# Long-convolution block: the shift's taps as 32-column products, a first stage without turns, and an inverse that overwrites the spectrum

## The chip, the core and the metric

The kernel runs on one core of one Trainium2 chip. The metric is the device time of one execution in microseconds (us). The kernel before takes 249.34 us (median of 3 runs, 249.3 to 249.93). The engines are PE (TensorE, with PEld for its weight loads), DVE (VectorE), ACT (ScalarE), POOL (GpSimd) and SP, which issues most transfers.

## The reference, cut to what matters

```python
def _A_ref(q, k, v, shift_k, ssm_k, ssm_D):          # q is layernorm(x)
    k_pad = jnp.pad(k, ((0, 0), (ks - 1, 0), (0, 0)))                  # ks = 4, S = 2048, D = 512
    k_shift = sum over t of k_pad[:, t:t + S, :] * shift_k[:, ks - 1 - t]
    kv = k_shift * v
    y = irfft(rfft(kv, 2 * S) * rfft(ssm_k, 2 * S))[:, :S, :]          # a causal convolution per channel
    return q * (y + kv * ssm_D)

def _B_ref(x, w1, b1, w2, b2):                        # an MLP, 512 -> 1376 -> 512
    return gelu(layernorm(x) @ w1 + b1) @ w2 + b2

x = A_q
for _ in range(2):
    x = x + _A_ref(layernorm(x), k, v, shift_k, ssm_k, ssm_D)
    x = x + _B_ref(layernorm(x), w1, b1, w2, b2)
```

The convolution y depends on k, v, shift_k, ssm_k and ssm_D alone, so both layers use the same y. The kernel computes it once.

## The kernel before, in words

The program has two parts. The **head** computes y and the first MLP group's first product; the **steady part** runs 8 groups (two layers of four) of 4 x 128 tokens, each as 44 products `ph` (L735), their gelu on ACT (L737) and 44 products `po` (L769). Only the head is changed, apart from names and from which token stands on which partition.

In the head the 2048 tokens are split into 32 high values a and 64 low values b. A transform over a (32 points, odd frequencies k = 0..31) comes first, then a twiddled transform over b for each k. The steps have names that the text uses; each product step fills one of four PSUM buffers `p` of 128x1024 numbers, and its evacuation (the same name with an `e`) copies that buffer to SBUF on ACT (L215) or DVE (L217):

- `kT` (L439) turns three of the four channel groups of k on PE, channels to partitions. `kv` (L521) then applies the four taps as products with diagonal matrices DG: 6 steps of 32 products, each with all 128 columns of the array; the turned k is the stationary operand, so tokens come out on partitions. `kvm` (L527) multiplies by v on DVE. The fourth channel group gets its taps on POOL instead (L453, L455, L460, L464).
- `U..S` (L303) is the transform over a of u = kv, 16 products of 256 columns for each of four channel groups. Its result must be turned before the second transform: `U..T`, 16 PE transposes a step (L335) for three groups, and two transposing transfers (L282) for the fourth.
- `KS` (L390) and `K2` (L403) are the same two transforms of ssm_k. KS uses whole products, 4 a step; K2 uses products with 64 rows in pairs (rows 0 to 63 and 64 to 127), 8 a step. The swapped copy of the spectrum that the complex product needs is made by 8 transfers (`sa`, `sb`, SBUF to SBUF).
- `X` (L551) is the second transform of u, `T` (L566) the product with the spectrum on DVE into buffers T, and `V` (L575) the inverse over k2, with T as the stationary operand.
- The inverse over k needs the result turned once more: two channel groups on PE (`TC`, `TD`, L610), two by transposing transfers `Z` (L622). `Y` (L642) is the last product, 32 products of 512 columns with the matrix GP.
- The tail: for the first group of tokens g (L669, L670) gates and adds on DVE, h (L237 to L243) takes statistics, p (L249) the power on POOL, b (L254) applies them, LT (L650) turns, and M (L698, gelu in L706) is the first MLP product, in three units of 1, 1 and 2 token blocks.

The order on every engine is written by hand: the string ORDER lists all steps as `name.engine` and PSUM slot, and each engine's instructions are emitted in that order, so an engine waits at its next step even if a later one is ready. Transfers are issued in the same way from SP's queue. `wm` steps (L420) are products on a table, which keep PE busy.

Of the kernel before, what the change touches and what calls it, by code (L numbers as in the profile page):

```python
# [9 lines left out]
BF16 = mybir.dt.bfloat16  # L10
# [8 lines left out]
lSK.S wm2.P2 bS.P2 wm0.P1 bSe.A dg0.D dg1.A dg2.A lk0.S lk1.S lh1.S kT0.P2 bSK.P1 bSKe.A kT0e.D kT1.P0 kT2.P3 lh113.S lb1.S lx0.S kT1e.D kT2e.A kT3.P1 wm1.P0 bB.P2 bBe.A lv0.S s00.A lv1.S kT3e.D kv10.P3 kvm10.D kv00.P1 U1S0.P30 kv01.P2 kvm00.D U1S1.P1 U0S0.P01 U1S0e.D lK01.S kg0.G kv11.P3 lK00.S kg1.G U0S0e.A kvm01.D U0S1.P0 s01.G U0S1e.A U0S3.P2 U1S1e.D kvm11.D U0S3e.A kv20.P1 kd0.P0 lK11.S lK10.S kvm20.D kd0e.A U1S3.P3 U0S2.P2 U1S3e.A U0S2e.D KS11.P0 KS11e.A KS01.P1 KS30.P3 KS01e.A lW.S KS00.P2 KS00e.A KS30e.D KS10.P0 KS31.P1 KS10e.D kv21.P3 kvm21.D KS31e.A kd4.P1 kd4e.A KS20.P0 KS21.P2 KS20e.A KS70.P1 KS21e.D KS51.P3 KS41.P0 KS70e.A KS51e.A KS60.P2 KS60e.A KS41e.D KS40.P1 KS61.P3 KS40e.D lX.S KS71.P0 KS50.P2 U1S2.P1 KS71e.D KS61e.A KS50e.A U1S2e.A U2S0.P32 U2S0e.D K25.P0 K25e.A K27.P2 K24.P1 K24e.A K23.P3 K21.P0 K21e.A K27e.D K26.P2 U2S1.P1 K26e.A K23e.D U2S1e.D K20.P3 K28.P0 K20e.A K22.P2 K22e.A K212.P1 K28e.D K215.P3 K215e.A lM.S K212e.D sa1.S sb1.S sa0.S K214.P0 K29.P2 K29e.A K213.P1 U0T0.P3 K214e.D K213e.A K210.P0 K210e.A sb0.S K211.P2 U0T1.P1 s02.D K211e.A U2S3.P0 U0T0e.D U2S3e.A U0T1e.D ka1.G kg2.G ka2.G kg3.G X00.P30 ka3.G kgm.G U3S0.P21 U3S0e.D U2S2.P1 X00e.A X01.P01 lH.S U2S2e.A U1T0.P3 U3S1.P2 T00.D0 U3S3.P1 X01e.A U1T1.P0 sb3.S U1T0e.D X10.P30 U3S1e.A U3S3e.A sa3.S X02.P22 T01.D1 X10e.A U2T0.P1 sb2.S U1T1e.D T10.D2 U3S2.P3 U2T0e.D X02e.A sa2.S X12.P01 V00.P2 U3S2e.A T02.D0 V10.P30 X12e.A X03.P10 V00e.A X03e.A V01.P0 V01e.A X20.P22 T12.D2 X20e.A U3T0.S V12.P1 X11.P01 X11e.A V10e.D lx.S V02.P3 U2T1.P2 T03.D1 X13.P00 T20.D2 V12e.A V02e.A T11.D0 V03.P1 U2T1e.D X13e.A V03e.A X30.P32 T13.D1 V11.P0 X30e.A V11e.D X23.P21 V13.P1 X23e.A U3T1.S V13e.A T30.D0 X22.P30 X22e.A T23.D1 V20.P01 X21.P22 ly.S X21e.A V20e.A V30.P12 X32.P31 T22.D2 T21.D0 X31.P20 V22.P0 X32e.A V21.P3 X31e.A V30e.D X33.P12 V22e.A Z01.S Z00.S X33e.A V23.P2 T32.D2 V23e.A T31.D0 V32.P0 V31.P1 T33b.D1 V33b.P2 T33a.D2 V31e.D Z11.S Z10.S V21e.A V32e.A V33a.P3 Z03.S V33ae.A TC0a.P0 TC0b.P1 Z13.S TC0ae.A TC0be.A w4.S V33be.D TD0b.P3 TD0a.P0 TD0ae.D TC3.P2 TD0be.A Y00.P0 Y01.P3 Y00e.A Y01e.A TC3e.D g00.D w1.S Z02.S TC1.P1 TC1e.A g01.D h00.D Y02.P2 Y32.P0 TC2.P3 Y02e.A h01.D Y32e.A Y10.P1 Y10e.A p00.G w3.S b00.D g02.D p01.G LT0.P2 LT0e.A Y12.P0 Y12e.A M0b.P1 M0be.A TC2e.A h02.D M0a.P2 b01.D LT1.P1 Y30.P0 LT1e.A p02.G b02.D LT2.P3 LG1.D LT2e.D M1a.P1 M0ae.A M1ae.A M1b.P2 M1be.A M2a.P3 M2ae.A M2b.P1 M2be.A M2c.P2 M2ce.A Y30e.A Z12.S w2.S Y20.P3 Y22.P1 Y20e.A Y22e.A  # L19
# [10 lines left out]
def _make_tables():  # L30
# [4 lines left out]
    F = np.zeros((128, 2, 128))  # L35
    G = np.zeros((128, 2, 128))
    for x in range(2):
        for bh in range(2):
            rows = 4 * a + 2 * bh + x
            F[rows, x, bh * 64:bh * 64 + 32] = np.cos(psi)  # L40
            F[rows, x, bh * 64 + 32:bh * 64 + 64] = np.sin(psi)
            for i, p in enumerate(rows):
                G[bh * 64:bh * 64 + 32, x, p] = np.cos(psi[i]) / 64
                G[bh * 64 + 32:bh * 64 + 64, x, p] = np.sin(psi[i]) / 64
# [3 lines left out]
    M = np.zeros((128, NA, 2, 128))  # L48
    for k in range(NA):
        phi = 2 * np.pi * (((k + 0.25) * b / 2048)[:, None] + np.outer(b, k2) / NB)  # L50
        c, s = np.cos(phi), np.sin(phi)
        for bh in range(2):
            cb, sb = c[bh * 32:bh * 32 + 32], s[bh * 32:bh * 32 + 32]
            r, i = bh * 64, bh * 64 + 32
            W[r:r + 32, k, 0:64] = cb
            W[r:r + 32, k, 64:128] = sb
            W[i:i + 32, k, 0:64] = -sb
            W[i:i + 32, k, 64:128] = cb
            for q, sign in ((0, 1.0), (64, -1.0)):
                M[q:q + 64, k, 0, r:r + 32] = sign * cb.T / 32  # L60
                M[q:q + 64, k, 0, i:i + 32] = -sign * sb.T / 32
                M[q:q + 64, k, 1, r:r + 32] = sb.T / 32
                M[q:q + 64, k, 1, i:i + 32] = cb.T / 32

# [4 lines left out]
    q = p % 32  # L69
    M = M[ri][:, :, :, p - q + 16 * (q // 4 % 2) + 4 * (q // 8) + q % 4]  # L70
    GP = G[32 * (p % 4) + p // 4]
    F2 = F.reshape(128, 2, 2, 2, 32).transpose(0, 3, 2, 1, 4).reshape(128, 256)
    KF = np.stack([np.cos(psi), np.sin(psi)], axis=2).reshape(32, 64)
    F = np.concatenate([F2, np.kron(np.eye(4), KF)], axis=1)
# [30 lines left out]
def kernel(ctx: ExitStack, tc: tile.TileContext, A_q, A_k, A_v, A_shift_k, A_ssm_k, A_ssm_D,  # L105
                 B_x, B_w1, B_b1, B_w2, B_b2, out):
    nc = tc.nc
    P = 128
# [741 lines left out]
```

## Time and profile before

| | us |
|---|---|
| device time, median of 3 runs | 249.34 |
| time of the execution that was profiled | 249.34 |
| its span, first to last instruction | 247.6 |
| its head, to the first `po` product that belongs to the steady rhythm | 101.4 |
| time outside the span | 1.74 |
| busy in the span: PE, DVE, ACT, POOL | 236.1, 171.9, 145.1, 54.5 |

The page gives busy time by engine, the span in 40 slices of 6.19 us, and the costliest groups of instructions. A PE instruction's listed duration contains its way through the array, so products that follow each other overlap; how fast PE works is read from the distance between starts, or from a whole run of them in the chain of waits. The granted clock is 0.997 over the span.

### The profile page before, as it was taken

Reading aid. Unit: us, or ns where it says so; the run is one execution under the profiler, and the core shown is the slowest. Engines: PE = TensorE matmul, PEld = TensorE weight load, DVE = VectorE, ACT = ScalarE, POOL = GpSimd, SP = SyncE. Lnnn points to the kernel's source line nnn. Section 1 sums busy time; section 2 is a strip of 40 time slices with the busy share of each in tenths; the row PEclk is TensorE's granted clock in tenths of the full one; section 3 lists DMA queues with packets and bytes.
Section 4 is the critical chain, followed back from the end, with each engine's and each line's share of the span. In section 5 each row is a group of like instructions: output and inputs, shape, how many; then the busy total and the mean of one; then the engine's idle time right before and its main releaser. Section 6 shows DMA issues by size and latency. Waiting matters only on the chain.

```text
span 247.6 us, 4783 instructions
## 1 busy us (share of the span) xinstructions
PE 236.1 (95%) x1918; PEld 146.4 (59%) x1929; DVE 171.9 (69%) x315; ACT 145.1 (59%) x218; POOL 54.5 (22%) x50
## 2 busy tenths in 40 slices
PE   4999999899999999999999999999999999999994
PEld 2689877699998688444444444444444444444443
DVE  1467899999997988878889898956956961021022
ACT  5596899899999899707406506505605604704800
POOL 2789999400000221111101111011011010000000
PEclk9999999999999999999999999999999999999998
DMA  6999994946999990040601204013016016011011
GB/s 244 351 292 173 264 437 192 394 175 120 218 254 179 282 260 5 0 85 1 87 0 38 47 3 85 0 23 63 3 44 127 0 45 127 1 42 42 3 42 42
DMA packets 50816, 29.65 MB, mean 120 GB/s; under 512 B 44675, under 2 KB 48488, under 8 KB 49258
## 3 DMA queue, kind: packets, MB, share of 16 engines
q1 hardware_dynamic: 50642, 29.21, 45.7%
q8 instruction: 15, 0.25, 0.4%
q10 hardware_dynamic: 152, 0.14, 0.2%
q14 instruction: 7, 0.06, 0.1%
HBM read 16.23 MB, written 2.10 MB: 74 GB/s over the span
## 4 chain that ended last, share of the span: by engine, by line
PE 72%; DVE 9%; ACT 9%; DMA 5%; issue 2%; POOL 0%; ACTq 0%; DVEq 0%; POOLq 0%
PE po L769 31%; PE ph L735 27%; ACT arena L215 3%; DMA arena<-in_A_v_dram 3%; ACT xb L215 3%; PE p L521 3%; DVE arena L217 3%; ACT ZT L215 2%; DMA arena<-in_A_ssm_D_dram 2%; PE p L698 2%; PE p L303 2%; DVE arena L254 2%; PE p L403 1%; PE p L335 1%; PE p L575 1%
## 5 line engine op out<-in xcount | busy, mean ns | idle before, releaser
L737 ACT ACTIVATE arena<-ph,B 128x512 bf16<-128x512 f32 (+1 forms) x77 | 52.9, 687 | 78.6 <-PE ph L735 78.6
L769 PE MATMUL po<-arena 128*128 128x512 bf16 (+2 forms) x356 | 77.1, 372 | 0.4
L735 PE MATMUL ph<-arena 128*128 128x512 bf16 (+1 forms) x308 | 67.6, 379 | 0.0
L769 PEld LDWEIGHTS <-arena 128*128 128x128 bf16 (+1 forms) x363 | 35.4, 98 | 40.7
L774 DVE TENSOR_TENSOR arena<-po,arena 128x512 bf16<-128x512 f32 (+1 forms) x33 | 21.6, 672 | 44.6 <-PE po L769 44.5
L735 PEld LDWEIGHTS <-arena 128*128 128x128 bf16 (+1 forms) x308 | 30.8, 100 | 35.9
L215 ACT ACTIVATE arena<-p 128x1024 bf16<-128x1024 f32 (+7 forms) x44 | 40.6, 1005 | 3.6 <-PE p L383 1.2
L249 POOL TENSOR_TENSOR lrsm<-lrsm,mhalf 128x4 f32<-128x4 f32 (+2 forms) x10 | 9.1, 910 | 92.3 <-DVE lrsm L243 89.5
L237 DVE BATCH_NORM_STATS2 lstm<-arena 128x6 f32<-128x512 bf16 x32 | 20.0, 681 | 0.2
L215 ACT ACTIVATE ZT<-p 128x1024 bf16<-128x1024 f32 (+1 forms) x18 | 17.9, 1040 | 1.9 <-PE p L303 1.7
L566 DVE TENSOR_TENSOR T<-xb,arena 128x2048 bf16<-128x2048 bf16 (+1 forms) x17 | 18.9, 1153 | 0.0
L254 DVE TENSOR_SCALAR arena<-arena,lmvg,lrsg 128x512 bf16<-128x512 bf16 x32 | 12.9, 465 | 7.3 <-POOL lrsg L249 7.3
L249 POOL TENSOR_TENSOR lrsg<-lrsg,mhalf 128x4 f32<-128x4 f32 x8 | 8.1, 1012 | 44.6 <-DVE lrsg L246 44.6
L237 DVE BATCH_NORM_STATS2 lstg<-arena 128x6 f32<-128x512 bf16 x28 | 17.2, 677 | 0.0
L575 PE MATMUL p<-arena,T 128*128 128x128 bf16 x256 | 16.2, 219 | 0.6 <-ACT ZT L215 0.3
L215 ACT ACTIVATE xb<-p 128x1024 bf16<-128x1024 f32 x16 | 16.3, 1059 | 0.6 <-PE p L551 0.6
L217 DVE COPY arena<-p 128x2048 bf16<-128x2048 bf16 (+3 forms) x12 | 12.3, 1031 | 5.1 <-PE p L439 3.3
L575 PEld LDWEIGHTS <-T 128*128 128x128 bf16 x256 | 14.8, 98 | 1.1 <-issue 0.7
L453 POOL TENSOR_TENSOR T<-arena,SK 128x2048 bf16<-128x2048 bf16 (+3 forms) x4 | 15.0, 3760 | 1.3 <-ACT SK L215 1.1
L254 DVE TENSOR_SCALAR arena<-arena,lmvm,lrsm 128x512 bf16<-128x512 bf16 x32 | 11.5, 416 | 2.8 <-POOL lrsm L249 2.8
L217 DVE CAST arena<-p 128x1024 bf16<-128x1024 f32 x11 | 12.9, 1217 | 0.3
L217 DVE CAST ZT<-p 128x1024 bf16<-128x1024 f32 (+1 forms) x11 | 12.8, 1170 | 0.4 <-ACT arena L215 0.2
(80 smaller groups left out, 249.5 us busy)
## 6 DMA issues: line engine op xcount, KB each, us to landing
arena<-arena SPq DMA_DIRECT2D x8, 512.0 KB, 5.6
arena<-in_A_k_dram SPq DMA_DIRECT2D x2, 1024.0 KB, 6.2
arena<-in_A_v_dram SPq DMA_DIRECT2D x2, 1024.0 KB
arena<-in_A_ssm_k_dram SPq DMA_DIRECT2D x4, 512.0 KB, 12.1
arena<-tabM SPq DMA_DIRECT2D x1, 2048.0 KB
out_dram<-arena SPq DMA_DIRECT2D x15, 128.0 KB, 1.7
arena<-in_A_q_dram SPq DMA_DIRECT2D x1, 1536.0 KB, 6.8
arena<-in_B_w_dram SPq DMA_DIRECT2D x1, 1376.0 KB, 6.7
```

The source lines that it names most:

```text
L215: nc.scalar.activation(dst, src, AF.Copy)
L217: nc.vector.tensor_copy(dst, src)
L237: nc.vector.bn_stats(self.st[:, i, 0, :], x_t[:, GT * g + i, :] if src is None else src[:, i, :])
L249: nc.gpsimd.tensor_tensor(self.rs[:, a:b], self.rs[:, a:b], mhalf[:, a:b], ALU.pow)
L254: nc.vector.tensor_scalar(out=dst[:, i, :], in0=xs, scalar1=self.mv[:, i, 0:1], scalar2=self.rs[:, i:i + 1], op0=ALU.subtract, op1=ALU.mult)
L453: nc.gpsimd.tensor_tensor(m[:, t:NT, :], kn[:, 0:NT - t, c3], sk(t, NT - t), ALU.mult)
L566: eng.tensor_tensor(view(Tb[it["slot"]["T"]], [2, n, CW]), x2, kk, ALU.mult)
L575: nc.tensor.matmul(o[:, i, :], T[:, r, i, :], Mt[:, ka + i, 1 - r, :], start=r == 0, stop=r == 1)
L735: nc.tensor.matmul(o.rearrange("p (i t) -> p i t", t=P), W1t[:, ct, ft * P:ft * P + m], lt[:, a:b, ct, :], start=ct == 0, stop=ct == CT - 1)
L737: nc.scalar.activation(hT[0:m, ft, a * P:b * P], o, AF.Gelu_apprx_tanh, bias=B1[0:m, ft:ft + 1])
L769: nc.tensor.matmul(po[:, a:b], hT[0:m, ft, i * P:(i + 1) * P], W2t[0:m, ft, a:b], start=ft == 0, stop=ft == FT - 1)
L774: nc.vector.tensor_tensor(xs, po[:, a:b], xs, ALU.add)
```

## The change

Each part below replaces the part of the same letters above.

- **kT, kv, kvm.** All four channel groups are turned (128 transposes instead of 48). A tap is now four products of 32 columns, one for each channel group, that write PSUM partitions 0-31, 32-63, 64-95 and 96-127 (L427): 8 steps of 128 products instead of 6 steps of 32. The stationary operand takes every fourth column of the turned k. v is loaded in the matching layout, 16 transfers of 32 partitions in pieces of 256 bytes, where it was two transfers in pieces of 8 KB. The taps on POOL and the loads for them are gone.
- **U.** The transform over a takes u straight from that layout, as products with 64 rows and 128 columns (L443), 16 steps of 8, and writes what X reads. The turns of u and their transposing transfers are gone.
- **KS, K2.** KS uses products of 64 rows and 64 columns, 16 a step (L319), K2 products of 64 rows and 128 moving columns, 16 a step (L333). ssm_k is loaded in pieces of 256 bytes instead of 128.
- **X, T, V.** X has 64 rows a product (L466): 128 products with 128 moving columns for the first two channel groups and 256 with 64 for the others. T (L484) writes the product over the spectrum itself; 11 of its 16 steps run on DVE and 5 on POOL. V (L494) then takes that spectrum as its stationary operand, with every 32nd element as the next column.
- **Y.** The last product takes the place of the turns and of GP: 512 products with 32 rows and 32 columns (L518) in 12 steps, and two evacuating copies a step. Its table Yt is 1 MB; the 2 MB table M is gone.
- ssm_k is loaded first of the large inputs, ahead of k; KS for the second half of the channels runs before the taps. The tokens' partition order changes, in x's loads and in the stores of the result, with pieces of the same size.

The core of the diff (the tables and the memory plan are left out):

```diff
-                        for t in range(KS):
-                            tau = 8 * o2 + i - t
-                            w = kT[:, cc, tau, 2:2 + P] if tau >= 0 else kT[:, cc, tau + NT, 1:1 + P]
-                            nc.tensor.matmul(o[:, i, :], w, DG[:, cc, t, :], start=t == 0, stop=t == KS - 1)
+                    for t in range(KS):
+                        tau, sh = (n0 + i - t, bh) if n0 + i >= t else (n0 + i - t + NT, bh - 1)
+                        for g in range(CT):
+                            nc.tensor.matmul(po[32 * g:32 * g + 32, i, :], kT[:, g, tau, 2 + sh:2 + sh + 125:4], DG[:, g, t, :],
+                                             start=t == 0, stop=t == KS - 1)
...
-                    for i in range(4):
-                        nc.tensor.matmul(o[:, i, :], src[:, 4 * q + i, cs], Ft[:, 0:256], start=True, stop=True)
...
-                        nc.tensor.transpose(o[:, i, :], zk, IDt[:])
+                    rs = slice(64 * hf, 64 * hf + 64)
+                    for m in range(8):
+                        nc.tensor.matmul(o[:, m, :, :], uX[rs, 8 * q + m].rearrange("p r b -> p (r b)"), Ft[rs, 512:640],
+                                         start=True, stop=True)
...
-                        nc.tensor.matmul(o[:, m, :], Kd[:, s0:s0 + 2, :].rearrange("p s b -> p (s b)"), Ft[:, 256:512],
-                                         start=True, stop=True)
+                        for x in range(2):
+                            for e in range(2):
+                                for par in range(2):
+                                    rs = slice(64 * e, 64 * e + 64)
+                                    nc.tensor.matmul(o[64 * par:64 * par + 64, 4 * e:4 * e + 4, m, :], Kd[hf][rs, 2 * q + m, par, 64 * x:64 * x + 64],
+                                                     Ft[rs, 256 * x:256 * x + 256], start=x == 0, stop=x == 1)
...
-                        nc.tensor.matmul(o[:, i, :], Wt[:, k0 + i, :], chunk(ZX, cc)[:, k0 + i, :], start=True, stop=True)
+                        for r in range(2):
+                            for q in range(2):
+                                rs = slice(64 * q, 64 * q + 64)
+                                nc.tensor.matmul(o[:, 2 * nc2 * q:2 * nc2 * q + 2 * nc2, i, :], (Wt if r == q else Wx)[rs, k0 + i, :],
+                                                 Zx[hf][rs, 2 * (k0 + i) + r, 64 * g0:64 * g0 + 64 * nc2].rearrange("p (f c) -> p f c", c=32),
+                                                 start=r == 0, stop=r == 1)
...
-                        eng.tensor_tensor(view(Tb[it["slot"]["T"]], [2, n, CW]), x2, kk, ALU.mult)
+                    (nc.vector if it["eng"] == "D" else nc.gpsimd).tensor_tensor(kk, x2, kk, ALU.mult)
...
-                                nc.tensor.matmul(o[:, i, :], T[:, r, i, :], Mt[:, ka + i, 1 - r, :], start=r == 0, stop=r == 1)
+                                nc.tensor.matmul(o[:, i, :], spec[cc // 2]((16 * (cc % 2) + 8 * w) * K + 2 * (m0 + i), [[32, P]]), Vt[:, w, :],
+                                                 start=w == 0, stop=w == 1)
...
-                    for x in range(2):
-                        nc.tensor.matmul(o[:, i, :], GPt[:, x, :], V2[g][:, x, t0 + i, :], start=x == 0, stop=x == 1)
+                        for r in range(2):
+                            for bh in range(4):
+                                for jj in range(2):
+                                    rs, b = slice(64 * hh + 32 * jj, 64 * hh + 32 * jj + 32), 16 * bh + GT * g + t0 + t
+                                    nc.tensor.matmul(o[32 * bh:32 * bh + 32, jj, t, :], Yv[rs, b, r, :], Zb[rs, r, b, :],
+                                                     start=r == 0, stop=r == 1)
```

The first place is PE where the taps begin. Before, a tap on one channel group is one product (`DG` moves, the turned k in `arena` is stationary), and U's first stage (L303) stands between two kv steps:

```order
L521 LDWEIGHTS arena
L521 MATMUL p_120<-DG,arena 128x128
...
L303 LDWEIGHTS arena
L303 MATMUL p_120<-Ft,arena 128x256
...
L521 LDWEIGHTS arena
L521 MATMUL p_119<-DG,arena 128x128
```

In the change the turned k is in `ra`, ssm_k in `spec`; the shape of a tap's product reads 32x128, and after 128 of them the kd step (L307, L308) and KS steps (L319) follow where U stood:

```order
L319 LDWEIGHTS spec_65
L319 MATMUL p_118<-Ft,spec_65 64x4x64
L427 LDWEIGHTS ra
L427 MATMUL p_115<-DG,ra 32x128
...
L307 LDWEIGHTS IDt
L307 MATMUL p_118<-spec_64,IDt 128x32
L308 LDWEIGHTS Dx
L308 MATMUL p_118<-IDt,Dx 128x32
```

U moved behind all eight kv steps, and KS of the first half of the channels moved in between them.

The second place is DVE between the transforms and the inverse, where `xb` holds X's evacuated result. Before, T writes a buffer of its own, and copies of turned u stand between the T steps:

```order
L217 COPY arena<-p_118 128x16x128
L566 TENSOR_TENSOR T_99<-xb_98,arena 128x2048
L566 TENSOR_TENSOR T_101<-xb_97,arena 128x2048
L217 CAST ZT_93<-p_120 128x32x32
L566 TENSOR_TENSOR T_100<-xb_96,arena 128x2048
```

In the change T writes `spec` in place; casts of U (`ra<-p`) and K2 (`spec<-p`) stand there instead of the turned copies:

```order
L201 CAST spec_64<-p_115 128x2x4x128
L484 TENSOR_TENSOR spec_65<-xb_97,spec_65 128x8x256
L201 CAST xb_94<-p_117 128x1024
L201 CAST ra<-p_118 128x128x8
L201 CAST ra<-p_117 128x128x8
L484 TENSOR_TENSOR spec_65<-xb_94,spec_65 128x8x256
```

Five of the sixteen T steps are no longer on DVE but on POOL, and the copies of turned u have gone from here.

The third place is PE behind the last inverse step. Before, turns (L610) and last products (L642, 512 columns) alternate:

```order
L575 LDWEIGHTS T_101
L575 MATMUL p_120<-arena,T_101 128x128
L610 LDWEIGHTS ZT_94
L610 MATMUL p_117<-IDt,ZT_94 128x128
...
L642 LDWEIGHTS GPt
L642 MATMUL p_117<-arena,GPt 128x512
```

In the change one warming product (L351) and then 320 small products on `rb`, the inverse's result, stand there; 192 more follow between and behind the M steps:

```order
L494 LDWEIGHTS spec_64
L494 MATMUL p_116<-Vt,spec_64 128x128
L351 LDWEIGHTS Ft
L351 MATMUL p_118<-Ft 128x512
L518 LDWEIGHTS Yt
L518 MATMUL p_118<-rb,Yt 32x128
```

Nothing is turned any more between the last V step and Y.

543 lines of the change are left out of this document (214 added, 329 removed).

## Prediction

> **What bounds the kernel now.** I read the page first, then the chain of waits in order of time, then busy time by stage, then the groups by shape inside the head.
>
> ```profile
> PE 236.1 (95%) x1918; PEld 146.4 (59%) x1929; DVE 171.9 (69%) x315; ACT 145.1 (59%) x218; POOL 54.5 (22%) x50
> PE   4999999899999999999999999999999999999994
> DVE  1467899999997988878889898956956961021022
> ACT  5596899899999899707406506505605604704800
> GB/s 244 351 292 173 264 437 192 394 175 120 218 254 179 282 260 5 0 85 1 87 0 38 47 3 85 0 23 63 3 44 127 0 45 127 1 42 42 3 42 42
> ```
>
> PE is busy nearly everywhere, DVE and ACT only in the first 16 slices, the head. The chain shows where the head ends and how densely PE issues.
>
> ```profile
> 1.19 5.32 DMA arena<-in_A_ssm_D_dram
> 6.52 7.88 DMA arena<-in_A_v_dram
> ...
> 16.42 1.79 PE p L521 x32
> 18.20 0.87 PE p L303 x8
> ...
> 50.47 1.01 PE p L335 x16
> ...
> 78.44 0.28 ACT arena L215
> ...
> 101.37 9.51 PE po L769 x44
> 110.88 9.50 PE ph L735 x44
> ```
>
> From 101.37 on the chain is PE alone, 9.5 us for 44 products of 512 columns, eight times over. The change leaves that part as it is, so I take its 247.6 − 101.4 = 146.2 us over unchanged, and the 249.34 − 247.6 = 1.74 us outside the span. The profiled execution took the median, 249.34, so no correction is needed between the two. All that can move is the head's 101.4 us: up to 78.7 for the transforms (the last V evacuation ends there), then a tail of 22.7. The durations that the sum needs are these: a product of 128 columns follows another after 1.79/32 = 56 ns, one of 256 columns after 0.87/8 = 109 ns, a transpose whose stationary operand has a stride of 32 elements after 1.01/16 = 63 ns.
>
> ```profile
> 0.00:101.40 101.40, 93.91 (x1255) 80.38 (x1260) 83.51 (x105) 89.84 (x139) 41.42 (x37) 1.00 0.85 234
> 65.00:70.00 5.00, 4.83 (x85) 4.73 (x85) 5.00 (x6) 5.00 (x7) 0.00 (x0) 1.00 1.11 321
> ```
>
> Columns are PE, PEld, DVE, ACT, POOL, clock, DMA share and GB/s. Over the head PE, ACT and DVE are all nearly full, and from 50 to 75 us ACT and DVE have no idle time at all: there the evacuations set the pace, not PE. So neither one engine's saving nor one engine's loss counts fully; it depends on the stage.
>
> **The change part by part.** First the counts, from the groups by shape in the head (count, busy us, mean ns).
>
> ```profile
> L521 PE MATMUL p<-DG,arena 128*128 128x128 bf16 x192 | 11.7, 219 | 0.4 <-ACT arena L215 0.3
> L303 PE MATMUL p<-Ft,arena 128*128 128x256 bf16 x64 | 8.8, 273 | 0.5 <-DVE arena L527 0.4
> L335 PE MATMUL p<-IDt,ZT 128*128 128x128 bf16 x96 | 7.1, 227 | 0.0
> L390 PE MATMUL p<-Ft,arena 128*128 128x256 bf16 x64 | 8.0, 272 | 0.3
> L575 PE MATMUL p<-arena,T 128*128 128x128 bf16 x256 | 16.2, 219 | 0.6 <-ACT ZT L215 0.3 <-ACT xb L215 0.2
> L610 PE MATMUL p<-IDt,ZT 128*128 128x128 bf16 x64 | 4.7, 227 | 0.4 <-ACT ZT L215 0.3
> L642 PE MATMUL p<-arena,GPt 128*128 128x512 bf16 x28 | 7.5, 379 | 0.2
> L439 PE MATMUL p<-IDt,arena 128*128 128x128 bf16 x48 | 3.0, 219 | 0.0
> ```
>
> *The taps* are the large unknown. 192 whole products, 192 × 56 ns = 10.8 us, become 1024 products that use 32 of 128 columns. If four of them run beside each other, they cost 56/4 = 14 ns each, 14.3 us. If they run one after another, 56 ns each, 57.3 us. No row of before has column strips. Two rows are near:
>
> ```profile
> 10.70 0.42 PE L370 MATMUL p<-one,arena 1*128 1x1 bf16 x11
> 42.94 0.37 PE L403 MATMUL p<-arena 64*128 64x256 bf16 x2
> 43.06 0.36 PE L403 MATMUL p<-arena,Wt 64*128 64x256 bf16 x2
> 43.17 0.36 PE L403 MATMUL p<-arena 64*128 64x256 bf16 x2
> 43.48 0.71 PE L335 MATMUL p<-IDt,ZT 128*128 128x128 bf16 x8
> L370 PE MATMUL p<-one,arena 1*128 1x1 bf16 x11 | 0.4, 159 | 0.0
> ```
>
> K2's products with 64 rows start in twos every 0.11 us, the time of one with 256 columns: parts of the array do work beside each other. But the densest stream of load and product in the trace is the smallest one, 11 products of one column: (0.42 − 0.16)/10 = 26 ns from start to start. Nothing was streaming there, so this is what it costs PE to begin a product. I take **26 ns a product wherever the parts of the array would allow less**, because 1024 pairs behind each other are closer to that row than to a pair of long ones: 26.6 us. Both ends stay for the range.
>
> The Trainium skill's page "TensorE: Matmul & The Clock Gate" has both numbers: its Part 1 gives a floor of about 25 ns from start to start however small the product, and its Part 3 ("Measured speedup vs the span model") says that products in different tiles of the array start about 4 ns apart. The 26 ns row agrees with the first, the pairs at 42.94 with the second. By the first rule the taps would be about 26 us, by the second 14; no run here shows which holds for a long stream of column strips.
>
> *The rest of the front.* kT grows from 48 to 128 transposes, 128 × 56 = 7.2 us. KS: 256 products of 256 columns, four tiles, 109/4 = 27 ns, 7.0 us as before. Where the shape of the array's parts changes, PE empties: the turn at 43.48 starts 0.21 us behind the last L403 pair (0.11 later than that pair's stream lasts), so 0.1 us for each of 24 changes up to the last kv step, 2.4 us. The profile's start of PE:
>
> ```profile
> 3.12 0.61 PE L420 MATMUL p<-Ft 128*128 128x512 bf16 x1 [3.12 <-DMA Ft<-tabF]
> 5.40 1.84 PE L420 MATMUL p<-Ft 128*128 128x512 bf16 x4
> ```
>
> The warming ends at 7.24, and still will (7.4 with 16 bias columns instead of 12). To the end of the last kv step PE then has 7.4 + 7.0 (KS) + 7.2 (kT) + 26.6 (kv) + 3 K2 steps × 16 × 27 ns = 1.3 + 0.6 (kd, bias) + 2.4 = **52.5 us**. This covers the loads. SP's queue now begins with half of ssm_k, then k, the other half, v in 16 pieces, X, W:
>
> ```profile
> 7.39 16.80 SPq L352 DMA_DIRECT2D arena<-in_A_ssm_k_dram  x4
> DVE arena L527 <- DMA arena<-in_A_v_dram: 2.9, 1, 2.9
> ```
>
> Before, SP stood 16.8 us at ssm_k's 128-byte pieces, 2 MB. 256-byte pieces are half as many for the same bytes, and v brings the same number again, so I put both at 17 us, 2 MB of k at 5 us (the slices' 350 to 430 GB/s), x, X and W at 6.5: v has landed by about 28 us, W by 33. At 26 ns a product the fifth kv step ends after 30 us and K2 starts after 40, so PE hides it. Were the taps at 14 ns, the wait for W would return what they save beyond about 40 us; v's wait alone was 2.9 us.
>
> *The middle*, from the last kv step to the last V evacuation, is set by who copies.
>
> ```profile
> L215 ACT ACTIVATE arena<-p 128x1024 bf16<-128x1024 f32 x30 | 28.8, 1053 | 0.5 <-PE p L403 0.5
> L217 DVE CAST arena<-p 128x1024 bf16<-128x1024 f32 x11 | 12.9, 1217 | 0.3
> L566 DVE TENSOR_TENSOR T<-xb,arena 128x2048 bf16<-128x2048 bf16 x15 | 17.7, 1215 | 0.0
> L460 POOL TENSOR_TENSOR T<-T,T 128x2048 bf16<-128x2048 bf16 x3 | 12.2, 4065 | 0.2
> ```
>
> ACT has 7 K2, 10 U, 13 X and 13 V evacuations there: 43 × 1.053 = 45.3 us. DVE has 18 casts × 1.217 = 21.9, 11 T × 1.215 = 13.4, two kvm, x's normalisation and group 1's statistics, about 8: 43. POOL's five T take 20.3 beside them. PE has 13 K2 steps × 0.45, 128 U × 56 ns = 7.2, X 128 × 28 + 256 × 26 ns = 10.2, V 256 × 63 ns = 16.1 (its stationary operand now has the stride of the turns; it was 256 × 56 = 14.3), and 1.6 for changes of shape: 41. So PE's 3 to 5 us more for V and X lie beside ACT, and the middle is **45.3 us**. The removed turns of u (96 × 63 = 6.0 us of PE, six DVE and two ACT copies, two transfers) save nothing beyond that, since the 6 K2 and U copies come in their place: ACT's total over the head comes to 91 against 89.8, DVE's to 76 against 75.5 without the steady part's steps. T in place rather than into a buffer: no row shows it; it reads and writes as many elements, so 0, and 11 × 0.5 us at worst.
>
> *The tail.* 64 turns × 63 ns = 4.0 and 32 products of 512 columns × 9.5/44 = 6.9 us go, 512 products × 26 ns = 13.3 come (by eight tiles side by side 56/8 = 7 ns, 3.6 us). M and LT stay. PE hardly waits there (nines in its slices 13 to 16), so 22.7 + 13.3 − 10.9 = **25.1 us**.
>
> Sum: 52.5 + 45.3 + 25.1 = 122.9 for the head, against 101.4. I take 1 us off where K2's copies already run under the last kv step, 122: 249.34 + 20.6 = **270 us**.
>
> **The rivals.** (1) *The strips run fully beside each other*, as K2's pairs do: 14 ns a tap and 7 ns a Y product. The front is 52.5 − 12.3 = 40.2 us, the middle stays ACT's 45.3, the tail falls to the 22.7 that its chain over DVE and ACT needs: 108.2, so 249.34 + 6.8 = 256; with only the taps so, 258 to 262. For it: the pairs at 42.94. Against: no stream below 26 ns. The span-model rule of Part 3 of the page named above would give this case; the trace bears it out for two row tiles.
>
> (2) *Faster: PE is the bound all the way, and the strips are free.* With strips at full rate the removed PE work (10.8 + 7.0 + 6.0 + 7.0 + 14.3 + 4.0 + 6.9 + 2.7 = 58.7 for the rows above) meets 14.3 + 7.2 + 7.0 + 16.1 + 3.6 + 7.2 = 55.4, and the 2.9 us in which kvm waited for v are filled by KS: 249.34 − 3.3 − 2.9 = 243, at 246 if X and the shape changes return half. It decides at the pace of a tap: 6 us more on 1024 products is 6 ns, so above 20 ns it is gone. It also needs the copies to spread into the front, which ORDER does not do: U, X and V all come behind the last kv step.
>
> (3) *The strips run one behind another:* 57.3 instead of 26.6 us, about 300. K2's pairs speak against it.
>
> **How the numbers follow.** Forecast, 265 to 280: 0.48. Rival 1 with its mixtures (only taps, or only in part, beside each other), 250 to 265: 0.32. Rival 2, under 248.6: 0.12. Rival 3: 0.05. Between 248.6 and 250, a mixture of 1 and 2: 0.03; that is within 0.3% of 249.34, about what a measurement here can tell from no change. So faster 0.12, same 0.03, slower 0.85. The range 250 to 280 holds the forecast and rival 1 and leaves out 0.20.
>
> **What would show it.** The distance between taps: 26, 14 or 56 ns, so a kv step of 3.3, 1.8 or 7.2 us. The last kv step's end near 52 us, the last V evacuation's near 97, the first `po` near 122. ACT full between the first two of these and not before. V at 63 ns. Y steps at 26 ns a product. The forecast fails if kv takes under 2.5 us, or if ACT has gaps in the middle because a swap of the spectrum or POOL's last T (4.07 us each, two behind each other) arrives late, which would add up to 4 us.

## The result, and the profile after

The changed kernel takes **287.37 us** (median of 4 runs, 286.14 to 287.82) against 249.48 us (4 runs, 249.3 to 249.93): 1.1513 times as long, 95% interval 1.1491 to 1.1536. It became slower, as forecast, but by 38 us where 20.6 were worked out, and outside the range of 250 to 280. The profiled execution took 287.45 us, with a span of 285.5 us.

From the page of the changed kernel: totals, then the 40 slices (7.14 us each here), the granted clock, and one DMA queue (its packets, MB and share).

```profile
PE 249.0 (87%) x3732; PEld 159.3 (56%) x3740; DVE 181.8 (64%) x324; ACT 134.8 (47%) x203; POOL 42.5 (15%) x38
...
PE   5977838787689199789999999999999999999994
...
DVE  3545382398998994865888898977787695003012
ACT  3632331397858358749707136064071360640810
POOL 1000020003955700040111111111011001000000
PEclk9998995999868869759999999999999999999999
...
q8 instruction: 29, 0.48, 0.7%
```

Before, PE showed nines in nearly every slice of the head. Now no engine is full through it: PE has holes, ACT has threes in the front, DVE is full only around the slices in which POOL works too (10 to 14), and the clock, which was 1.00 over the head, dips. Queue q8 brings instructions: 29 packets of about 16 KB, one for each 256 of PE's 3732 + 3740 products and loads (29.2). Before there were 1918 + 1929, which is 15.0 times 256, and 15 packets. The runs below with fewer products keep to it: 23 packets for 5936 instructions of PE in x_split_t_dve_whole, 25 for 6448 in two_strips, 21 for 5424 in y_half.

Busy time by stage: front (to the end of the last kvm), middle (to the end of the last V evacuation), tail (to the first `po`). Columns are PE, PEld, DVE, ACT, POOL, clock, DMA share, GB/s.

```profile
0.00:58.50 58.50, 41.87 (x1480) 33.65 (x1480) 27.74 (x37) 22.48 (x28) 2.87 (x15) 0.91 0.66 177
58.50:116.30 57.80, 44.75 (x929) 41.94 (x930) 49.75 (x43) 40.39 (x42) 22.79 (x5) 0.85 0.51 160
116.30:138.60 22.30, 20.10 (x661) 17.61 (x662) 16.12 (x37) 16.99 (x53) 3.75 (x5) 0.77 0.01 3
```

The prediction had 52.5, 45.3 and 25.1, but its front ended with the last kv step on PE, which is over at 56.6 us (the entry at 55.55 below); the 1.9 us of the last kvm that follow belong to its middle. Counted its way, the front is 56.6 us, 4.1 over, the middle 59.7, 14.4 over, and the tail 22.3, 2.8 under. From the first `po` on it is 285.5 − 138.6 = 146.9 us, against 146.2, with the same 142 us of PE: the steady part is as it was.

The chain of waits, in order of time (start, length, what):

```profile
21.81 11.08 DMA lna<-in_A_q_dram
...
37.91 1.99 PE p L427 x128
...
40.69 3.41 issue
44.09 3.50 PE p L427 x122
...
55.55 1.04 PE p L427 x58
...
88.17 11.26 DVE spec L484 x3
...
138.56 0.32 PE po L647
```

Three things are new: a load of 0.5 MB that lands after 11.08 us, stretches of `issue` in which PE waits for nothing that the profile can name, and three T steps on DVE (L484) that last 11.26 us, where three took 3 × 1.215 = 3.6 before.

The groups by shape in the head (count, busy us, mean ns, idle time ahead and what ended it):

```profile
L484 DVE TENSOR_TENSOR spec<-xb,spec 128x2048 bf16<-128x2048 bf16 x11 | 24.9, 2289 | 0.7 <-ACT xb L199 0.6
L484 POOL TENSOR_TENSOR spec<-xb,spec 128x2048 bf16<-128x2048 bf16 x5 | 22.8, 4579 | 37.9 <-ACT xb L199 37.9
L427 PE MATMUL p<-DG,ra 128*32 128x128 bf16 x1024 | 20.3, 239 | 12.4 <-issue 10.1 <-DVE rb L434 2.3
L434 DVE TENSOR_TENSOR rb<-p,rb 128x1024 bf16<-128x1024 f32 x8 | 15.6, 1955 | 17.1 <-PE p L427 10.8 <-DMA rb<-in_A_v_dram 6.0
```

A T on DVE takes 2289 ns on average instead of 1215, a kvm 1955 instead of 1220. The taps take 20.3 us of work and 12.4 us of waiting, 10.1 of it `issue` in seven stops.

### The profile page after: what moved, and what is told of

It is laid out like the page before. It is cut to its first block, busy times and chain, and to the rows that moved or that the text cites. A ratio compares the mean times of both kernels' runs of the same rounds, so it can differ in the third digit from the quotient of the medians.

```text
span 285.5 us, 8361 instructions
## 1 busy us (share of the span) xinstructions
PE 249.0 (87%) x3732; PEld 159.3 (56%) x3740; DVE 181.8 (64%) x324; ACT 134.8 (47%) x203; POOL 42.5 (15%) x38
## 4 chain that ended last, share of the span: by engine, by line
PE 68%; DVE 11%; SPq 7%; issue 5%; DMA 4%; ACT 2%; DVEq 0%; ACTq 0%
PE po L647 27%; PE ph L613 23%; DVE spec L484 5%; PE p L494 4%; SPq L257 4%; PE p L576 4%; DMA lna<-in_A_q_dram 4%; PE p L427 4%; SPq L281 3%; DVE ra L201 2%; PE p L518 2%; ACT rb L199 2%; PE p L466 2%; PE p L333 1%; DVE rb L434 1%
## 5 line engine op out<-in xcount | busy, mean ns | idle before, releaser
L615 ACT ACTIVATE spec<-ph,B 128x512 bf16<-128x512 f32 (+1 forms) x77 | 52.8, 687 | 79.0 <-PE ph L613 78.9
L647 PE MATMUL po<-ra,spec 128*128 128x512 bf16 (+3 forms) x355 | 77.0, 372 | 0.4
L613 PE MATMUL ph<-ra,rz 128*128 128x512 bf16 (+1 forms) x308 | 67.6, 379 | 0.0
L647 PEld LDWEIGHTS <-spec 128*128 128x128 bf16 (+1 forms) x363 | 35.4, 98 | 40.5
L613 PEld LDWEIGHTS <-rz 128*128 128x128 bf16 (+1 forms) x308 | 30.8, 100 | 35.9
L652 DVE TENSOR_TENSOR rz<-po,rz 128x512 bf16<-128x512 f32 (+1 forms) x33 | 21.6, 671 | 44.9 <-PE po L647 44.9
L427 PE MATMUL p<-DG,ra 128*32 128x128 bf16 x1024 | 20.3, 239 | 12.4 <-issue 10.1
L484 POOL TENSOR_TENSOR spec<-xb,spec 128x2048 bf16<-128x2048 bf16 x5 | 22.8, 4579 | 37.9 <-ACT xb L199 37.9
L434 DVE TENSOR_TENSOR rb<-p,rb 128x1024 bf16<-128x1024 f32 x8 | 15.6, 1955 | 17.1 <-PE p L427 10.8
L427 PEld LDWEIGHTS <-ra 128*32 128x32 bf16 x1024 | 17.8, 116 | 15.1 <-issue 14.9
L494 PE MATMUL p<-Vt,spec 128*128 128x128 bf16 x256 | 19.2, 241 | 7.0 <-DVE rb L201 7.0
L484 DVE TENSOR_TENSOR spec<-xb,spec 128x2048 bf16<-128x2048 bf16 x11 | 24.9, 2289 | 0.7 <-ACT xb L199 0.6
L494 PEld LDWEIGHTS <-spec 128*128 128x128 bf16 x256 | 18.4, 153 | 7.6 <-issue 7.1
L219 DVE BATCH_NORM_STATS2 lstm<-rz 128x6 f32<-128x512 bf16 x32 | 20.0, 681 | 0.2
L199 ACT ACTIVATE xb<-p 128x1024 bf16<-128x1024 f32 x13 | 13.0, 1027 | 11.1 <-PE p L466 6.0
```

The lines of the kernel that those rows point to most:

```text
L199: nc.scalar.activation(dst, src, AF.Copy)
L219: nc.vector.bn_stats(self.st[:, i, 0, :], x_t[:, GT * g + i, :] if src is None else src[:, i, :])
L427: nc.tensor.matmul(po[32 * g:32 * g + 32, i, :], kT[:, g, tau, 2 + sh:2 + sh + 125:4], DG[:, g, t, :], start=t == 0, stop=t == KS - 1)
L434: nc.vector.tensor_tensor(uX[:, :, :, 8 * o:8 * o + 8], kk, v, ALU.mult)
L484: (nc.vector if it["eng"] == "D" else nc.gpsimd).tensor_tensor(kk, x2, kk, ALU.mult)
L494: nc.tensor.matmul(o[:, i, :], spec[cc // 2]((16 * (cc % 2) + 8 * w) * K + 2 * (m0 + i), [[32, P]]), Vt[:, w, :], start=w == 0, stop=w == 1)
```

## The experiments

Four theories are named in the expectations. **P**: DVE and POOL hold each other up where both work on T. **I**: PE waits for its own instructions, which come in blocks of 256. **Q**: in the front, DVE stands in its queue for the first piece of x, and kvm and PE behind it. **E**: a transfer whose source has 4 as its outermost count (all loads of x have, since the new order of tokens is four rows of 32 partitions) uses 4 of the 16 DMA engines. All results:

| run | against the change | us (median) | ratio to before, 95% interval |
|---|---|---|---|
| (the change) | | 287.37 | 1.1513 (1.1491 to 1.1536) |
| t_all_dve | all T on DVE | 285.38 | 1.1419 (1.1395 to 1.1442) |
| x_split | x in loads of 32 partitions | 287.19 | 1.1512 (1.1459 to 1.1564) |
| x_split_t_dve | both | 277.58 | 1.1146 (1.1105 to 1.1187) |
| whole_taps | whole products for the taps | 281.19 | 1.1275 (1.1238 to 1.1312) |
| x_split_t_dve_whole | all three | 266.69 | 1.0713 (1.0677 to 1.0749) |
| two_strips | x_split_t_dve, half the taps | 266.99 | 1.07 (1.0657 to 1.0743) |
| x_split_t_dve_vbig | x_split_t_dve, v in 4 KB pieces | 279.95 | 1.1236 (1.121 to 1.1262) |
| x_stats_late | x's statistics later | 292.83 | 1.1726 (1.1667 to 1.1785) |
| kvm_flat | kvm without strides | 286.83 | 1.1494 (1.1457 to 1.1531) |
| whole_flat | all three, kvm without strides | 266.4 | 1.0653 (1.0596 to 1.0709) |
| y_half | all three, half of Y | 262.32 | 1.0507 (1.0457 to 1.0558) |
| before_t_pool | the kernel before, five T on POOL | 260.78 | 1.0434 (1.039 to 1.0478) |

### T on POOL, and x's loads

*t_all_dve*: five entries of ORDER.

```diff
-T30.G ... T21.G ... T22.G ... T03.G ... T07.G
+T30.D ... T21.D ... T22.D ... T03.D ... T07.D
```

> All sixteen T steps on DVE, none on POOL; nothing else moves. Theory P (DVE and POOL slow each other when both run T): DVE's T falls from a mean of 2.29 us to about 1.22 each, 16 x 1.22 = 19.5 us instead of 24.9 us on DVE, PE's wait of 7.0 us ahead of V at 93.6 us goes, and the time falls by 9 to 13 us, to 274 to 278. Rival (T written over the spectrum is slow in itself): T stays near 2.3 us, 16 x 2.3 = 37 us on DVE, and the time rises by 5 us or more.

The group of T in this run:

```profile
L484 DVE TENSOR_TENSOR spec<-xb,spec 128x2048 bf16<-128x2048 bf16 x16 | 18.8, 1215 | 0.0
```

DVE's timeline where V ends (start, us, what, idle time ahead and what ended it):

```profile
100.72 1.22 DVE L201 CAST rb<-p 128x1024 bf16<-128x1024 f32 x1 [1.09 <-ACT rb L199]
111.55 2.47 DVE L219 BATCH_NORM_STATS2 lstg<-rz 128x6 f32<-128x512 bf16 x4 [9.61 <-DMA rz<-in_A_q_dram]
...
114.42 1.22 DVE L201 CAST rb<-p 128x1024 bf16<-128x1024 f32 x1
```

The durations bear P out: 16 T on DVE take 18.8 us, where 11 took 24.9, and not 37 as the rival had it. But the time fell by 2 us only, where 9 to 13 were expected. The second fence shows why: DVE is through with T early and then stands 9.61 us for x, whose statistics stand in DVE's order ahead of the last V cast (`rb`, 114.42). Y starts at 115.7, in the change at 116.3. A second wait lay under the first. The transfer itself (chain of waits):

```profile
78.18 33.35 DMA rz<-in_A_q_dram
```

and the DMA engines once the other loads are done, with share and GB/s in the last two columns:

```profile
104.00:110.00 6.00, 2.93 (x44) 2.59 (x42) 0.00 (x0) 3.76 (x4) 0.00 (x0) 1.00 0.26 84
```

A share of 0.26 is 4 of 16 engines. Hence theory E and the next run.

*x_split*: the three loads of x (first group, again for group 1, rest), each as four transfers of 32 partitions.

```diff
-rows(q_d, 0, GT)   # [[NT * D, 4], [4 * NT * D, 32], [1, GT * D]]
+for i in range(4):
+    nc.sync.dma_start(dst[32 * i:32 * i + 32, :], apf(q_d, (t0 + NT * i) * D, [[4 * NT * D, 32], [1, (t1 - t0) * D]]))
```

> The three loads of x are each issued as four transfers of 32 partitions, same bytes to the same places. Theory E (a transfer whose source has 4 as its outermost count keeps to 4 of the 16 DMA engines): x for group 0 lands about 4 us after its issue instead of 11, the last x load about 8 us after its issue instead of 33; DVE's wait of 5.2 us for x goes. Alone this gives 2 to 6 us, 281 to 285, since T on POOL still holds the middle. Rival (the queue is full of v's 256-byte pieces and x stands behind them): x lands as late as before, time within 1.5 us.

The same entry of the chain of waits, and what stands there a little later:

```profile
81.46 6.30 DMA rz<-in_A_q_dram
...
87.77 11.24 DVE spec L490 x3
```

Busy time while that transfer runs, with the same columns:

```profile
82.00:87.00 5.00, 4.38 (x79) 4.08 (x78) 4.21 (x4) 2.59 (x3) 0.49 (x1) 0.50 1.00 228
```

All 16 engines are busy (1.00) at 228 instead of 84 GB/s, and x is there 24 us earlier than in t_all_dve (87.8 against 111.5). A single transfer is not slow in itself. The kernel before loaded the same 1.5 MB in one, whose source has 128 as its outermost count (size, and us from issue to landing, at the end of the row):

```profile
arena<-in_A_q_dram SPq DMA_DIRECT2D x1, 1536.0 KB, 6.8
```

The time is the same (287.19): now T on POOL alone holds the end of V. E is right on the transfer and missed on the time, as P did.

*x_split_t_dve*: both edits together.

> Both: x loads in four transfers each and all T on DVE. In t_all_dve DVE stood at group 1's statistics until the last x load landed at 111.5 us, which is why that run gained only 2 us. If so, the two together give what neither gives alone: 10 to 15 us, 272 to 277. If the last x load was not what held t_all_dve, the sum of the single effects, 281 or more.

277.58 us, 9.8 us less than the change, just short of the 10 to 15 expected, where the two alone gave 2.0 and 0.2. The middle, with the columns of the stages above:

```profile
57.50:105.80 48.30, 42.02 (x929) 39.33 (x930) 43.15 (x47) 40.38 (x42) 0.00 (x0) 0.93 0.61 192
```

The middle falls from 57.8 to 48.3 us, with the same work on ACT (40.4). Two waits that covered each other were worth 2.0 and 0.2 us singly and 9.8 us as a pair.

*before_t_pool*: the kernel before, with five T given to POOL, to see P without anything else of the change.

```diff
-T01.D ... T02.D ... T20.D ... T11.D ... T23.D
+T01.G ... T02.G ... T20.G ... T11.G ... T23.G
```

> The kernel before with five of its T steps (T01, T02, T20, T11, T23) on POOL. Theory P: DVE's T steps and its bf16 copies that run beside a T on POOL take 2 us and more instead of 1.2, POOL's take 4.1 to 4.6 us, and V waits for POOL's: 254 to 264. Rival (POOL's and DVE's T do not touch each other): DVE's T stay at 1.22 us, and the time moves by what V waits for POOL alone, 249 to 254.

The groups of T:

```profile
L566 DVE TENSOR_TENSOR T<-xb,arena 128x2048 bf16<-128x2048 bf16 x10 | 21.2, 2137 | 2.7 <-ACT xb L215 2.6
L566 POOL TENSOR_TENSOR T<-xb,arena 128x2048 bf16<-128x2048 bf16 x5 | 20.7, 4150 | 14.2 <-PE p L575 8.1 <-ACT xb L215 6.1
```

DVE's timeline (start, us, what):

```profile
54.88 2.29 DVE L566 TENSOR_TENSOR T<-xb,arena 128x2048 bf16<-128x2048 bf16 x1 [0.26 <-ACT xb L215]
57.10 1.21 DVE L217 COPY arena<-p 128x2048 bf16<-128x2048 bf16 x1
58.39 3.87 DVE L566 TENSOR_TENSOR T<-xb,arena 128x2048 bf16<-128x2048 bf16 x1
```

POOL's, over the same time:

```profile
51.98 4.11 POOL L566 TENSOR_TENSOR T<-xb,arena 128x2048 bf16<-128x2048 bf16 x1 [6.09 <-ACT xb L215]
57.12 4.06 POOL L566 TENSOR_TENSOR T<-xb,arena 128x2048 bf16<-128x2048 bf16 x1 [1.03 <-PE p L575]
```

POOL's steps end at 56.09 and 61.18. DVE's T that began under them end at 57.17 and 62.26, in both cases 1.08 us later, though POOL's steps covered 1.2 us of the first and 2.8 us of the second. So DVE's T is not slowed in proportion to the overlap; it does next to nothing until POOL's is over. In the change itself it is the same: POOL's pair of T ends at 98.35, the last of the three DVE steps at 99.43. The copy from PSUM at 57.10, which ran beside a T of POOL, took its usual 1.21 us. The time went up by 11.1 us (260.78 against 249.69 beside it).

*x_stats_late* tests Q: the first group's statistics of x moved behind kvm5.

```diff
-s00 s01 ... kvm5
+kvm5 s00 s01
```

> The statistics of x (s00, s01) come behind the last kvm in DVE's order instead of between the second and the third. Theory Q (DVE stands in its queue for x, 5.2 us, and kvm, PSUM and PE wait behind it): the last kv step ends 4 to 6 us earlier and the time falls by 4 to 6 us, to 281 to 283. Theory I (instruction blocks pace the front, and PE's wait for kvm was 2.3 us in all): 0 to 2.3 us.

292.83 us, 5.5 us more. Q falls: DVE's next wait is for v, which has landed only by 34.2 us, the last kv step ends where it did, and statistics placed later stand between kvm and the copies (2.9 us of DVE from 58.5 on). x_split says the same: x is early there, DVE does not wait for it, and the last kv step ends at 56.8. The chain's entry:

```profile
27.35 6.87 DMA rb<-in_A_v_dram
```

### The taps and PE's instructions

PE's timeline of the changed kernel, where the taps begin:

```profile
20.70 0.31 PE L427 MATMUL p<-DG,ra 128*32 128x128 bf16 x7 [1.75 <-issue]
...
21.20 1.87 PE L427 MATMUL p<-DG,ra 128*32 128x128 bf16 x118
25.07 0.36 PE L427 MATMUL p<-DG,ra 128*32 128x128 bf16 x10 [2.00 <-issue]
25.36 1.48 PE L319 MATMUL p<-Ft,spec 64*64 64x256 bf16 x32
26.77 2.54 PE L427 MATMUL p<-DG,ra 128*32 128x128 bf16 x86
29.62 0.81 PE L427 MATMUL p<-DG,ra 128*32 128x128 bf16 x42 [0.31 <-issue]
```

Between one stop and the next lie 7 + 1 + 1 + 118 = 127 products (the two ones are the kd step's) and 10 + 32 + 86 = 128: with their weight loads 254 and 256 instructions, the size of one of q8's blocks. PE starts again at 20.70, 25.07 and 29.62, a block every 4.4 to 4.6 us here. The rival to that reading is that narrow products, of any number, hold PE up. The next three runs tell the two apart.

*whole_taps* takes away three quarters of the taps' instructions: one whole product for four strips.

```diff
-for g in range(CT):
-    nc.tensor.matmul(po[32 * g:32 * g + 32, i, :], kT[:, g, tau, 2 + sh:2 + sh + 125:4], DG[:, g, t, :], ...
+nc.tensor.matmul(po[:, i, :], kT[:, i % CT, tau, 2:2 + P], DG[:, i % CT, t, :], ...
```

> Each tap is one product with all 128 columns on contiguous columns of the turned k, instead of four products with 32 columns: 32 products a kv step instead of 128, the same time in the array (32 x 56 ns = 1.8 us). It computes taps on other tokens than the reference wants. Theory I (PE waits for its own instructions, one block of 256 at a time): PE's idle time put down to issue ahead of L427 falls from 10.1 us to under 2, the last kv step ends near 47 us instead of 56.6, and the time falls by 7 to 10 us, to 277 to 280. Rival (the front waits for v, x and kvm): the last kv step still ends at 54 us or later, and the time moves by less than 3 us.

281.19 us, 6.2 us less, a little under the 7 to 10 expected. No `issue` is left ahead of the taps, but 6.9 us of waiting for kvm, which stands behind x's statistics on DVE, took its place, and the last kv step ends at 50.2, not 47. *x_split_t_dve_whole* is the same on top of both edits above, where no other wait takes the gain back:

> Also with whole 128-column taps, a quarter of the tap products (taps of other tokens than the reference's). Theory I: with x and T out of the way the instruction blocks are the largest wait left on PE before 57 us; 7 to 11 us less than x_split_t_dve, 263 to 268. Rival: v's landing at 34 us holds the front instead, less than 4 us.

266.69 us, 10.9 us less than x_split_t_dve. The taps' group in x_split_t_dve, where all their idle time is `issue`:

```profile
L433 PE MATMUL p<-DG,ra 128*32 128x128 bf16 x1024 | 20.1, 238 | 11.5 <-issue 11.5
```

The same group with whole products:

```profile
L432 PE MATMUL p<-DG,ra 128*128 128x128 bf16 x256 | 15.7, 219 | 1.6 <-DVE rb L439 1.6
```

An entry of that run's chain of waits, in the front:

```profile
29.65 8.49 DMA Wt<-tabW
```

The 11.5 us are gone, the clock over the front is 1.00 (0.94 there), and the front, with the last kvm, ends at 45.5 instead of 57.5 us; W, landed at 38.1, is now on the chain.

*two_strips* keeps the narrow products and halves their number: half of the channels get no taps.

```diff
-for g in range(CT):
+for g in range(2):
```

> x_split_t_dve with only two of a tap's four products, so half the channels get no taps: 512 products instead of 1024, still 32 columns wide, and 16 in a row per strip as before, so the array needs the same 1.8 us a kv step if strips run beside each other. Theory I (256 PE instructions a block): 1024 fewer instructions of the 1536 that whole taps saved, so 6 to 10 us less than x_split_t_dve's 277.6, 268 to 272, with issue waits ahead of the taps under 4 us instead of 11.5. Rival (narrow products are slow in themselves): 0 to 3 us less.

266.99 us, 10.6 us less than x_split_t_dve, a little more than the 6 to 10 expected. The group of the taps:

```profile
L433 PE MATMUL p<-DG,ra 128*32 128x128 bf16 x512 | 15.8, 220 | 1.3 <-DVE rb L440 1.3
```

A kv step on the chain of waits:

```profile
32.49 1.98 PE p L433 x64
```

The same shape, and no `issue` ahead of the taps (one stop of 1.35 us remains in the front, ahead of a KS step): the number of instructions is the cause, not the narrowness. And 64 products on two strips need 1.91 to 1.98 us, as 128 on four do (1.99), or 32 whole ones (1.89 and 1.91 in x_split_t_dve_whole): four strips share one pass of 60 ns.

*x_split_t_dve_vbig*: v's 16 transfers of 256-byte pieces replaced by 4 with pieces of 4 KB, in case v's small pieces delay the blocks.

```diff
-nc.sync.dma_start(vx[32 * g:32 * g + 32, 16 * o:16 * o + 16, :], apf(v_d, 16 * o * D + g * P, [[NB * D, 32], [D, 16], [1, P]]))
+nc.sync.dma_start(vx[:, 16 * o:16 * o + 16, :].rearrange("p b c -> p (b c)"), apf(v_d, 16 * o * P, [[NB * P, P], [1, 16 * P]]))
```

> x_split_t_dve with v loaded in pieces of 4 KB, four transfers instead of sixteen, in an order of tokens and channels that is not the reference's. v then lands by 20 to 24 us instead of 34. If v's small pieces hold the front, 4 to 8 us less than x_split_t_dve; if the instruction blocks do (theory I), less than 2.5 us.

279.95 us, 2.4 us more. From its chain:

```profile
19.24 3.39 issue
...
26.64 2.82 issue
```

The stops stay and the first ones grow, though DVE no longer waits for v at all. v's pieces are not what holds the front. What sets the pace of a block was not separated further; that loads share the way with the blocks cannot be all of it, since the stop of 1.76 us in the tail, shown under *y_half*, comes at a DMA share of 0.00.

### Strides and the tail

*kvm_flat* lets kvm read and write without the order that U wants (u is then not in the reference's order).

```diff
-v = vx[:, 8 * o:8 * o + 8, :].rearrange("p b (r m) -> p m r b", r=2)
-kk = view(...).rearrange("p b (r m) -> p m r b", r=2)
-nc.vector.tensor_tensor(uX[:, :, :, 8 * o:8 * o + 8], kk, v, ALU.mult)
+nc.vector.tensor_tensor(place(rb, [8, P], (16 + 2 * o) * K), kk, v, ALU.mult)
```

> kvm reads PSUM and v and writes u with neighbouring elements, in an order that is not the reference's. If the strides of kvm's operands are what makes it 1.96 us instead of 1.22, it falls to 1.22. The time falls by 0.7 us (the last kvm, which U waits for) to 2 us: DVE waited 10.8 us for PE ahead of these steps, so the others lie in slack.

Each kvm takes 1223 instead of 1955 ns, 5.9 us of DVE in all, and the time, 286.83, cannot be told from the change's: DVE has slack there.

*whole_flat* is the same edit on x_split_t_dve_whole, where the taps no longer wait:

> x_split_t_dve_whole with kvm on neighbouring elements (order of u not the reference's). With the instruction blocks out of the front, kvm's 8 x 0.7 us on DVE count more than in kvm_flat, where they gave nothing: 1 to 5 us less than 266.7. If v's landing (DVE waited 4.6 us for it) holds the front, under 1 us.

266.4 us, with a ratio whose interval overlaps that of x_split_t_dve_whole: inconclusive. The ratios are 0.6% apart, 1.5 us, and their intervals leave room for anything from 0 to some 3 us.

*y_half*, also on x_split_t_dve_whole, computes one of the two halves of each sum in Y, 256 products instead of 512.

```diff
-for r in range(2):
+for r in range(1):
```

> x_split_t_dve_whole with only the first of the two halves of each last product (the sine part is left out): 256 products of 32 rows and columns instead of 512, evacuations unchanged. If instruction blocks hold the tail (issue waits of 1.8 and 1.2 us among Y there), 2 to 5 us less than 266.7. If the tail is set by the chain through DVE, ACT and the M products, under 1 us.

262.32 us, 4.4 us less, or 17 ns for each of the 256 products that went. The group of Y in x_split_t_dve_whole and in this run:

```profile
L523 PE MATMUL p<-rb,Yt 32*32 32x128 bf16 x512 | 6.6, 243 | 4.3 <-issue 2.9 <-ACT rb L199 0.9 <-ACT spec L199 0.5
L523 PE MATMUL p<-rb,Yt 32*32 32x128 bf16 x256 | 3.9, 251 | 2.6 <-ACT spec L199 1.7 <-ACT rb L199 0.9
```

The `issue` in Y, 2.9 us, is gone. The array needs about 8 ns for one product: in x_split_t_dve_whole 64 of them that meet no stop take 0.77 us, of which 0.25 is the last one's own length, so (0.77 − 0.25)/63 (PE's timeline, with one of the two stops for blocks that follow):

```profile
95.89 0.77 PE L523 MATMUL p<-rb,Yt 32*32 32x128 bf16 x64 [0.25 <-ACT spec L199]
...
99.25 1.25 PE L523 MATMUL p<-rb,Yt 32*32 32x128 bf16 x77 [1.76 <-issue]
```

## Why the prediction missed, step by step

**The middle: the failed step is "POOL's five T take 20.3 beside them".** They take 22.8, and not beside: DVE's eleven T cost 24.9 us instead of 13.4. POOL's work was priced by POOL's duration alone. That two such steps cannot run at once is shown by t_all_dve's durations and by before_t_pool, where five T on POOL bring 11.1 us into a kernel that has nothing else of the change. The Trainium skill's page "SBUF — State Buffer", section "Who interferes with whom", states it: a DVE instruction with two inputs in SBUF contends with a GpSimd instruction that reads SBUF, over ports that it calls an exclusive lock, while a DVE instruction with at most one input there, outside the two-port modes, does not contend. The 1.08 us behind POOL's end and the 1.21 us of the copy, whose input is in PSUM, agree.

**Also in the middle: x's loads were taken at nothing for their new order.** The first was counted at 6.5 us together with two tables, the other two not at all. The words "in x's loads and in the stores of the result, with pieces of the same size" were read as no change. The pieces are the same, but the source's outermost count is now 4, and the load of 1.5 MB took 33.35 us, where the kernel before took 6.8. The Trainium skill's page "DMA: Bandwidth & Descriptors", section "Why a DMA increments its semaphore by 16 and not by 1", gives the rule: the number of engines is the largest up to 16 that divides the outermost counts of both sides; the share of 0.26 agrees. With both items removed, in x_split_t_dve, the middle is 50.3 us from the last kv step on (55.5 to 105.8), so together they are 9.4 of its excess of 14.4. The other 5 us are not explained in full: the last kvm, 1.9 us, stands on the chain ahead of U, where the sum put it beside ACT's copies. ACT's work in the changed kernel's middle was 41.7, less than the 45.3 counted, and no engine is full.

**The front: 26 ns a tap was right as a total and wrong as a mechanism.** The step between taps is 1.99/128 = 15.5 ns in an undisturbed kv step, what rival 1 said (14). So the failed step here is "26 ns a product wherever the parts of the array would allow less": the 26 ns of the eleven-product row are no floor for products on different strips. By the prediction's own mark, "if kv takes under 2.5 us", the forecast should have failed towards 256. It did not, since the taps stopped: 20.3 us of work and 12.4 of waiting (10.1 for instructions, 2.3 for a kvm that stood behind x's statistics), 32.7 in place of 26.6. That the sum of a price too high and a wait left out came near is luck. The excess of 6.1 is more than the front's 4.1, so the front's other terms came out about 2 us under; they were not taken apart. The row of eleven small products said nothing of the stops: eleven products fit into one block. What the prediction missed is the supply over a long stream, 2048 instructions for the taps, a block of 256 every 4.4 to 4.6 us in the rows above. The Trainium skill's page "Runtime: NRT & Kernel Launch", section "Instruction fetch mechanics", has the blocks of 256 and calls crossing into the next one mostly hidden; here it was not, with stops up to 3.41 us.

**The clock was taken as 1.00 throughout.** Busy time in the kv step ahead of the stop of 3.41 us, in the one behind it, and in the first M step of the tail, 32 products (the clock is the third number from the end):

```profile
37.91:39.80 1.89, 1.89 (x128) 1.82 (x127) 1.89 (x1) 0.00 (x0) 0.00 (x0) 1.00 0.99 412
44.10:47.50 3.40, 3.40 (x122) 3.22 (x121) 0.00 (x0) 0.00 (x0) 0.00 (x0) 0.50 0.09 34
124.55:128.07 3.52, 3.52 (x36) 3.52 (x35) 1.87 (x6) 1.08 (x2) 2.23 (x3) 0.50 0.02 5
```

The two kv steps run the same products: 1.99 us for 128 at a clock of 1.00, 3.50 us for 122 at 0.50. That gap in PE was paid twice, once while it lasted and once behind it. Not every gap is: behind the stop of 2.00 us at 25.07 the clock was 0.60 over the next 4.2 us, but behind the stops of 1.75 us (20.70) and 1.29 us (55.55) and behind the wait of 2.31 us for kvm (37.91) it was 1.00. What decides it was not separated.

**The tail: 22.3 instead of 25.1.** Y was taken at 26 ns a product. The array gives 8 ns; by y_half's time a product costs 17, with 2.9 of the 4.4 us in stops. The 22.3 are near rival 1's 22.7 for the tail, but partly by luck: neither sum had the clock, which was 0.77 over this stage, nor the stops.

**Right**: that the change makes it slower, that the steady part stays, and V's pace (80 products in 5.29 us in x_split_t_dve, 66 ns each, where 63 were taken). kvm's longer time lies beside other work in the change, as far as kvm_flat can tell. That PE's added work in V and X does so too, and that the turns' removal saves nothing on the path, was not tested. The case that "POOL's last T (4.07 us each, two behind each other) arrives late", up to 4 us, named the right place, but not that POOL's T holds up DVE's.

**The balance.** Of the 38 us, the pair of T on POOL and x's loads is 9.8, the taps' instruction stream 10.9, half of Y's products 4.4; these are steps in the order in which the runs took them, and in another order they could split otherwise. Some 13 us remain between y_half's 262.3 and the kernel before. They are not separated. The step "v has landed by about 28 us, W by 33" was early by 5 to 6 us in both (34.2 in x_stats_late, 38.1 in x_split_t_dve_whole), and in the latter the last kv step ends at 43.6, 3.4 over rival 1's 40.2; that the loads make this difference is only argued. No version that was run comes below the kernel before.

## What to carry to other kernels

Count instructions, not only array time: products that run beside each other are cheap for the array and each still costs a load and a product, and a stream of thousands was paced here by how fast blocks of 256 arrive. Moving work to an idle engine is free only if the two engines can run such instructions at once, so look for a row where they overlap. When an edit that visibly shortens its rows moves the time little, look for the second wait that ends at the same place, and remove both.

## What the runs showed of the hardware

- Column strips do run side by side: 128 products of 32 columns in 1.99 us, 64 on two strips in 1.91 to 1.98, 32 whole ones in 1.89 to 1.91. Products of 32 rows and 32 columns follow each other at about 8 ns where nothing stops them.
- With products that short, PE stopped between blocks of 256 instructions: seven times in the taps, 0.3 to 3.4 us each and 10.1 us in all, and once for 1.76 us in a tail with a DMA share of 0.00. Where PE came to the end of a block late, behind another wait or at half clock, it did not stop.
- A T on DVE that begins under one on POOL ends 1.08 us behind POOL's end, however long the two overlapped (a T alone takes 1.215 us); a copy from PSUM beside POOL's T took its usual 1.21 us.
- The same 1.5 MB load with 4 as the outermost count of its source: 33.35 us, at a DMA share of 0.26 where no other load ran; with 128 as that count 6.8 us in one transfer; in four transfers of 32 partitions 4.28 to 6.30 us from the last one's issue to its landing.
- A stop of PE of 3.4 us was followed by 3.4 us at half clock; stops of 1.75 and 1.29 us and a wait of 2.31 us were followed by a clock of 1.00.
- A product on DVE from PSUM with strided operands takes 1955 ns for 128x1024, without strides 1223 ns.
